# A Fourier-mixing and feed-forward kernel: first batch of x loaded in partition halves on two queues, column copies on another engine, last spill split by rows

## The chip, the cores and the metric

The kernel runs on one core of one Trainium2 chip. The core has a matrix engine (TensorE, PE in the profile; its weight loads are PEld), a vector engine (VectorE, DVE), a scalar engine (ScalarE, ACT), GpSimd (POOL) and SyncE (SP), which here only starts transfers. Engines run in parallel, each works through its own instruction stream in order, and semaphores make one wait for another. Transfers are started from the streams of SP, ACT or POOL and run on 16 shared DMA engines. The metric is the device time of one execution in microseconds (us), as the median over several runs.

## What is computed

```python
batch, seq, dim = (8, 3008, 256)
X = np.fft.fft(x, axis=1)
X = np.fft.fft(X, axis=2)
x = X.real.reshape(24064, 256)
h = x @ w_in                                  # 256 -> 2048
g = h * (1.0 / (1.0 + np.exp(-1.702 * h)))
out = g @ w_out                               # 2048 -> 256
```

A two-dimensional Fourier transform of each of eight batches, its real part, and a two-layer network on every row, all in float32.

## The kernel before

The Fourier transform is done with matrix products. The sequence of 3008 = 47 * 64 is split: a first stage mixes over 47 groups of rows, its result goes out to memory (`Td`, the "spill", line 289) and comes back with another axis on the partitions (`t4`, the "fill", line 295), and a second stage (`stage2`, line 314) mixes over 64. The transform over the 256 columns is folded into the weights: `fold_w` (line 418) multiplies w_in with a cosine table and leaves `wcs`. The main loop then runs 384 steps (8 batches, 3 blocks of rows, 2 halves, 8 pairs of 128 hidden units), each with the products of `hidden` (line 448), an activation, and the products of `product` (line 515). The next batch's first stage runs between the steps of the batch before it.

The first batch has no batch before it, so its first stage stands alone at the start of the kernel, and the change is there. It goes like this.

- `w0`, the mixing table (128 partitions, 800.5 KB), is loaded from ACT's stream (line 589) and scaled into a second copy `w0o` by ACT (line 600).
- `x[0]` lies in `xt` as 32 slots of 256 columns. Partitions 0 to 63 hold one half of the rows (`half` 0) and 64 to 127 the other. It is loaded by `load_first` (line 225) in four calls of eight slots each: slots 0 to 8, 24 to 32, 8 to 16, 16 to 24. One call starts four transfers of 32 partitions and 256 KB: partitions 0-31, 32-63, 64-95, 96-127, in that order. Fourteen of the 16 start from SP and two (slots 24 to 32, half 0) from ACT.
- Behind them SP starts `small` (the other tables), then the weight pieces `raw` `in 0` and `in 1` of 1 MB each (lines 594, 339).
- `warm(7)` (line 278) issues products whose result nobody reads.
- `fold_first(g)` (line 233) works on four slots: ACT copies two columns of each (line 235, 128 x 8 elements), DVE makes sums and differences of columns (line 237, two instructions). The order of the g is 0, 7, 1, then 6, 2, then 5, 3, then 4.
- `mix_first(k)`, k = 0 to 3 (line 240), is the mixing on PE: 32 products of 64 x 64 weights in two phases (64 entries in the profile), with two one-column copies on ACT between the phases (line 248). The first phase of mix k cannot begin before the sum and the column copy of the last g that it needs: g = 1, 2, 3, 4 for k = 0, 1, 2, 3. Afterwards ACT copies the two result banks back to `xt` (line 264).
- After k = 1, 2, 3 `spill` writes finished slots to `Td`, one transfer for each half of the partitions. The last one starts from SP and ACT. Then `fill(0, 0, 4)` reads rows 0 to 512 of `Td`, which are what rows m = 0 to 16 of every mix produced.
- Then the first weight piece is rounded. `bounds` puts two passes on ACT (lines 362, 363) and one on POOL (line 360), `round_in` three on DVE (lines 373 to 376), `finish_in` one on POOL (line 380). Four more `warm` products follow, and `fold_w(0)`, the correction `rotate` (lines 301, 302), and `stage2` of block 0, with which the main loop starts. The other seven weight pieces are rounded between the first steps of the main loop.

The order on every engine is the order in which the code issues instructions (`manual_schedule`). Eight semaphores are used in rotation for transfers started from SP and ACT together, so a ninth such transfer waits until the first has landed, and so on. Transfers started from POOL have eight others.

Of the kernel before, what the change touches and what calls it, by code (L numbers as in the profile page):

```python
# [35 lines left out]
NJ = NB // 2  # L36
NM = 48
# [9 lines left out]
def view(ap, offset, *dims):  # L47
    return bass.AP(ap.tensor, ap.offset + offset, [list(d) for d in dims])


def free(ap, offset, *dims):
    return bass.AP(ap.tensor, ap.offset + offset, [list(ap.ap[0])] + [list(d) for d in dims])
# [57 lines left out]
def kernel(ctx: ExitStack, tc, x, w_in, w_out, tab1, tab2, out):  # L110
    nc = tc.nc
    B, S, D = x.shape
    DF = w_in.shape[1]
    H = D // 2
# [17 lines left out]
    Td = [nc.dram_tensor(f"Td{b}", (NG * 128, D), F32, kind="Internal").ap() for b in range(B)]  # L132
# [17 lines left out]
    def bank(name):  # L150
        return psm.tile([128, 512], F32, tag="mm", name=name)
# [6 lines left out]
    xt = xp.tile([128, NJ, D], F32, tag="x", name="xt")  # L158
# [63 lines left out]

    room = {}

    def load_first(lo, hi, engines):
        for half in range(2):
            for g in range(2):
                eng, p = engines[2 * half + g], 64 * half + 32 * g
                eng.dma_start(out=xt[p:p + 32, lo:hi, :].rearrange("p j d -> p (j d)"),
                              in_=view(x, (NB * (NA - 32) * g + NJ * half + lo) * D, [NB * D, 32], [1, (hi - lo) * D]))  # L230

    def fold_first(g):

        t, e = xt[:, 4 * g:4 * g + 4, :], room[g]
        nc.scalar.copy(free(e, 0, [D, 4], [H, 2]), free(t, 0, [D, 4], [H, 2]))
        for at, op in ((1, ALU.add), (H + 1, ALU.subtract)):
            nc.vector.tensor_tensor(e[:, :, at:at + H - 1], t[:, :, 1:H], free(t, D - 1, [D, 4], [-1, H - 1]), op=op)

    def mix_first(k):


        ks = k, 7 - k
        ps = [bank("ps1") for _ in ks]
        for phase in range(2):
            if phase:

                for n in range(2):
                    nc.scalar.copy(af2[:, n:n + 1], ps[n][:, D + n * (H + 1):D + n * (H + 1) + 1])
            for at in range(4)[::-1 if phase else 1]:
                r, even = divmod(at, 2)  # L250
                for half in (phase, 1 - phase):
                    n = half ^ phase
                    for c in range(2):
                        jj = 4 * ks[n] + 2 * r + c
                        c0, c1 = (0, H + 1) if even ^ half ^ phase else (H + 1, D)
                        slot, first = ((NB - jj) % NJ if half else jj), c0 == 0
                        w, m = (w0o, jj) if jj and not first else (w0, jj or ENDS[1 - first])
                        rows_ = slice(64 * half, 64 * half + 64)
                        nc.tensor.matmul(ps[n][64 * c:64 * c + 64, r * D + c0:r * D + c1], lhsT=mat(w, m, rows_),  # L259
                                         rhs=room[slot // 4][rows_, slot % 4, c0:c1], start=(phase == 0 and at == 0),  # L260
                                         stop=(phase == 1), skip_group_check=True)
        for n in range(2):
            to = placed(ks[n])
            nc.scalar.copy(xt[:, to:to + 2, :].rearrange("p j d -> p (j d)"), ps[n][:])  # L264

    def placed(k):
        return 2 * k if k < 4 else 16 + 2 * k
# [6 lines left out]
    def warm(n):  # L274

        ps = bank("warm")
        for _ in range(n):
            nc.tensor.matmul(ps[:], lhsT=wcs[0][:, 0:128], rhs=wcs[0][:, 0:512], start=True, stop=True)

    def spill(b, ks=None, engines=(nc.sync, nc.sync)):  # L280

        for c, eng in enumerate(engines):
            src, at = xt[64 * c:64 * c + NM], 16 * c * D
            if ks is None:
                eng.dma_start(out=view(Td[b], at, [NJ * D, NM], [1, 16 * D]),
                              in_=src[:, 0:16, :].rearrange("p q d -> p (q d)"))
                continue
            (k0, n), k1 = ks, 8 - sum(ks)
            eng.dma_start(out=view(Td[b], at + 2 * k0 * D, [NJ * D, NM], [2 * (k1 - k0) * D, 2], [1, 2 * n * D]),
                          in_=free(src, placed(k0) * D, [(placed(k1) - placed(k0)) * D, 2], [1, 2 * n * D]))  # L290

    def fill(b, a0=0, a1=NG):
        if a0 == 0:
            t4t[b] = tp.tile([128, NG, D], F32, tag="t4", name="t4")
        nc.sync.dma_start(out=t4t[b][:, a0:a1, :], in_=Td[b].rearrange("(a p) d -> p a d", p=128)[:, a0:a1, :])
# [41 lines left out]
    def load_in(n, eng):  # L337
        t = raw["in", n] = cv.tile([128, 1024, 2], U32, tag="raw", bufs=3, name="raw")
        eng.dma_start(out=t[:].rearrange("p (i f) w -> p i (f w)", i=2),
                      in_=w_in[:, n * 512:(n + 1) * 512].bitcast(U32).rearrange("(i p) f -> p i f", p=128))  # L340

    def load_out(n, eng):
        t = raw["out", n] = cv.tile([128, 1024, 2], U32, tag="raw", bufs=3, name="raw")
        eng.dma_start(out=t[:].rearrange("p (f n) w -> p f (n w)", f=4),
                      in_=w_out[4 * n * 128:(4 * n + 4) * 128, :].bitcast(U32).rearrange("(p f) n -> p f n", p=128))
# [3 lines left out]
    def bounds(key, first=False):  # L349


        hi, lo = raw[key][:, :, 1].bitcast(F32), raw[key][:, :, 0]
        g = sp.tile([128, 1024], F32, tag="s", bufs=3, name="g")
        m = cv.tile([128, 1024], F32, tag="m", name="m")
        r = cv.tile([128, 1024], U32, tag="r", bufs=2, name="r")
        if first:
            nc.vector.tensor_tensor(g[:], hi, hi, op=ALU.mult)
        else:
            nc.scalar.activation(g[:], hi, ACTF.Square)
        nc.gpsimd.tensor_scalar(m[:], hi, scalar1=TOP, scalar2=-TOP, op0=ALU.min, op1=ALU.max)  # L360

        nc.scalar.activation(r[:].bitcast(F32), lo, ACTF.Copy, scale=2.0 ** -29, bias=2.0 ** 23)  # L362
        nc.scalar.activation(r[:], r[:].bitcast(F32), ACTF.Copy, bias=-2.0 ** 23)  # L363
        pre[key] = g, m, r
# [36 lines left out]
    def finish_in(n):  # L401
        last["in", n]()
# [184 lines left out]
    nc.vector.memset(wcs[0][:, 0:512], 1.0)  # L587
    nc.vector.memset(ones[:], 1.0)
    nc.scalar.dma_start(out=w0, in_=tab1[:, 0:n0 + 1])
    load_first(0, 8, (nc.sync,) * 4)  # L590
    load_first(24, 32, (nc.scalar, nc.scalar, nc.sync, nc.sync))
    load_first(8, 16, (nc.sync,) * 4)
    load_first(16, 24, (nc.sync,) * 4)
    nc.sync.dma_start(out=small[:], in_=tab2)
    load_in(0, nc.sync)
    load_in(1, nc.sync)
    warm(7)

# [2 lines left out]
    for k, need in enumerate(((0, 7, 1), (6, 2), (5, 3), (4,))):  # L601
        for g in need:
            fold_first(g)
        mix_first(k)
        if k:
            spill(0, ((0, 2), (2, 1), (3, 1))[k - 1], (nc.sync, nc.scalar if k == 3 else nc.sync))
    fill(0, 0, 4)
    load_out(0, nc.sync)
    bounds(("in", 0), True)
    round_in(0)  # L610
    finish_in(0)
    warm(4)
    bounds(("in", 1))
    fold_w(0)
    fill(0, 4, NG)
# [13 lines left out]
    n = len(steps)  # L629
# [17 lines left out]
    for b in range(B):  # L647
        t0 = b * NBLK * NF
        late = 0 if b else 3
        if b + 2 < B:  # L650
            at(t0 + 10, turn, b + 2)
        if b + 1 < B:
            for c in range(NCH):
                at(t0 + 7 + 2 * c + late, fold1, b + 1, c, nc.gpsimd)
                if c % 2:
                    at(t0 + 8 + 2 * c + late, mix1, b + 1, c // 2)
            at(t0 + 24 + late, spill, b + 1)
            at(t0 + 29 + late, fill, b + 1)
            if b + 2 < B:
                at(t0 + 33 + late, load_x, b + 2)  # L660
            at(t0 + 36 + late, rotate, b + 1)
        for blk in range(NBLK):
            nxt = (b, blk + 1) if blk + 1 < NBLK else (b + 1, 0)
            if nxt[0] < B:
                at(t0 + blk * NF + 8, stage2, *nxt)
                at(t0 + blk * NF + 12, nyquist, *nxt)
# [49 lines left out]
```

## Time and profile before

| | us |
|---|---|
| median of 7 runs | 1939.94 (1939.35 to 1941.69) |
| the profiled execution, its own time | 1938.24 |
| its span in the profile | 1936.2 |
| PE busy | 1909.4 (99% of the span) |
| PEld / POOL / DVE / ACT busy | 1671.8 / 755.1 / 1410.0 / 674.9 |
| mean granted PE clock | 0.992 of full |
| first result of the last mix of batch 0 copied (line 264) | 36.22 |
| first products of the main loop (line 448) | 50.41 |

Except for the first 90 us or so, PE is busy almost without a gap. The profile has several views that are used below: the chain of work that ended last (start, length, engine, tile, line), the table of stages (start:end, length, then the busy time of PE, PEld, DVE, ACT and POOL with the number of instructions in brackets, then the granted PE clock, the mean busy share of the DMA engines, and GB/s moved), and the timeline (start, length from first start to last end, engine, line, operation, out<-in, count, and in brackets the idle time before it with what ended it).

### The profile page before, as it was taken

The numbers are of one execution on the slowest core, as the hardware profiler recorded it, in microseconds if no ns is written. First come the engines' busy times: TensorE is split into PE (matmuls) and PEld (weight loads), VectorE is DVE, ScalarE is ACT, GpSimd is POOL, SyncE is SP. The second block draws the span as 40 slices with busy tenths as digits, with TensorE's granted clock in tenths as the row PEclk, the third lists the DMA queues.
The fourth block names the chain that finished last, engine by engine and source line by source line (L and its number), as shares of the span: only waits on it lengthen the run. The fifth ranks groups of instructions, "written<-read, shape, count | busy, mean of one in ns | idle before, by whom it ended". The sixth has DMA issues, their size and how long they took to land.

```text
span 1936.2 us, 29491 instructions
## 1 busy us (share of the span) xinstructions
PE 1909.4 (99%) x10820; PEld 1671.8 (86%) x10820; DVE 1410.0 (73%) x2924; ACT 674.9 (35%) x936; POOL 755.1 (39%) x1045
## 2 busy tenths in 40 slices
PE   7899999999999999999999999999999999999998
PEld 4598888988889888898889888898888988889887
DVE  3777777777778667877777777777777777777776
ACT  3733333333333333333333333333333333333332
POOL 1565223642245322462225522355223643223222
PEclk7999999999999999999999999999999999999999
DMA  8740460227203362025522262221720223202201
GB/s 235 205 70 11 91 82 13 49 51 116 17 12 58 49 109 17 20 51 93 65 24 49 32 102 41 25 49 43 115 24 13 18 45 59 17 12 27 17 12 22
DMA packets 145520, 104.53 MB, mean 54 GB/s; under 512 B 105443, under 2 KB 128259, under 8 KB 143681
## 3 DMA queue, kind: packets, MB, share of 16 engines
q1 hardware_dynamic: 143360, 100.84, 31.1%
q10 hardware_dynamic: 2016, 1.81, 0.3%
q8 instruction: 86, 1.41, 0.3%
q14 instruction: 58, 0.47, 0.1%
HBM read 59.36 MB, written 48.01 MB: 55 GB/s over the span
## 4 chain that ended last, share of the span: by engine, by line
PE 96%; DMA 1%; POOL 1%; issue 1%; DVE 1%; ACT 1%; ACTq 0%; POOLq 0%; DVEq 0%
PE po L515 59%; PE pa L448 17%; PE pb L448 17%; PE ps L210 1%; PE ps L314 1%; DMA xt<-in_x_dram 1%; PE ps L259 1%; PE psw L418 0%; POOL wst L380 0%; POOL wo L380 0%; PE ps L214 0%; ACT xt L264 0%; POOL m L360 0%; ACT r L362 0%; ACT r L363 0%
## 5 line engine op out<-in xcount | busy, mean ns | idle before, releaser
L489 POOL TENSOR_TENSOR s<-h 128x256 f32<-128x256 f32 (+1 forms) x376 | 270.0, 718 | 1094.1 <-ACT h L477 1029.0
L515 PE MATMUL po<-s,wt 128*128 128x256 f32 (+1 forms) x2256 | 599.7, 375 | 0.0
L452 ACT COPY v<-pa 128x512 f32<-128x512 f32 (+1 forms) x384 | 222.0, 578 | 1062.8 <-PE pa L448 1062.8
L462 DVE TENSOR_TENSOR h<-v,pb 128x512 f32<-128x512 f32 (+1 forms) x384 | 259.1, 675 | 398.2 <-PE pb L448 393.5
L515 PEld LDWEIGHTS po<-s,wt 128*128 128x128 f32 x2256 | 428.6, 190 | 48.3
L515 PE MATMUL po<-h,wo 128*128 128x256 f32 (+1 forms) x1632 | 469.7, 375 | 0.1
L477 ACT ACTIVATE h<-h 128x1024 f32<-128x1024 f32 (+1 forms) x384 | 400.8, 1044 | 18.0 <-DVE h L472 15.3
L448 PE MATMUL pa<-pq,wcs 128*128 128x256 f32 (+1 forms) x1536 | 393.8, 379 | 2.6 <-ACT wcs L420 1.3
L448 PE MATMUL pb<-pq,wcs 128*128 128x256 f32 (+1 forms) x1536 | 387.9, 375 | 2.1 <-DVE dif L465 1.8
L515 PEld LDWEIGHTS po<-h,wo 128*128 128x128 f32 x1632 | 310.0, 190 | 36.0 <-issue 0.5
L448 PEld LDWEIGHTS pa<-pq,wcs 128*128 128x128 f32 x1536 | 286.8, 190 | 51.2 <-issue 11.2
L465 DVE SCALAR_TENSOR_TENSOR dif<-nb,af,pb 128x256 f32<-128x256 f32 (+1 forms) x768 | 328.3, 469 | 2.2 <-DMA af<-row 2.2
L448 PEld LDWEIGHTS pb<-pq,wcs 128*128 128x128 f32 x1536 | 291.5, 190 | 36.2 <-DVE dif L465 2.2
L490 POOL TENSOR_TENSOR s<-h 128x256 f32<-128x256 f32 (+1 forms) x376 | 276.4, 735 | 0.0
L472 DVE TENSOR_TENSOR h<-pa,dif 128x512 f32<-128x512 f32 (+1 forms) x448 | 265.4, 604 | 13.2
L515 PE MATMUL po<-s,wo 128*128 128x256 f32 (+1 forms) x752 | 220.3, 375 | 0.0
L515 PE MATMUL po<-h,wt 128*128 128x256 f32 (+1 forms) x752 | 220.3, 375 | 0.0
L493 DVE TENSOR_TENSOR s<-h,s 128x256 f32<-128x256 f32 (+1 forms) x376 | 206.0, 548 | 12.9
L492 DVE TENSOR_TENSOR s<-s,h 128x256 f32<-128x256 f32 (+1 forms) x376 | 179.2, 476 | 4.3 <-POOL s L489 4.3
L515 PEld LDWEIGHTS po<-s,wo 128*128 128x128 f32 x752 | 142.9, 190 | 16.1
L515 PEld LDWEIGHTS po<-h,wt 128*128 128x128 f32 x752 | 142.9, 190 | 16.1
L320 DVE STREAM_TRANSPOSE pq<-ps 128x256 f32<-128x256 f32 x96 | 34.6, 417 | 59.4 <-PE ps L314 59.4
(66 smaller groups left out, 741.5 us busy)
## 6 DMA issues: line engine op xcount, KB each, us to landing
out_dram<-os SPq DMA_DIRECT2D x284, 64.0 KB
Td<-xt SPq DMA_DIRECT2D x14, 768.0 KB
t<-Td SPq DMA_DIRECT2D x7, 1536.0 KB
xt<-in_x_dram SPq DMA_DIRECT2D x14, 512.0 KB
xt<-Xr SPq DMA_DIRECT2D x14, 512.0 KB
nb<-pq SPq DMA_DIRECT2D x23, 256.0 KB
out_dram<-os SPq DMA_DIRECT2D x96, 56.0 KB
Xr<-in_x_dram SPq DMA_DIRECT2D x7, 752.0 KB
```

Of the source, the lines that this page charges most:

```text
L320: nc.vector.transpose(free(pq[:], cs * 512 + u * RUN, [256, 2], [NU * RUN, 4], [1, RUN]), free(ps[u][:], cs * 256, [128, 2], [32, 4], [1, ...
L448: nc.tensor.matmul(ps[:, i * 256:i * 256 + n], lhsT=wcs[cs][:, f * 128:(f + 1) * 128], rhs=pq[:, cs, ks], start=True, stop=True)
L452: nc.scalar.copy(two(v[:], n), two(pa[:], n))
L462: nc.vector.tensor_tensor(two(h[:], n), two(v[:], n), two(pb[:], n), op=ALU.add)
L465: nc.vector.scalar_tensor_tensor(dif[:, i * 256:i * 256 + n], nb[:, ks], af2[:, f:f + 1], pb[:, i * 256:i * 256 + n], op0=ALU.mult, op1=AL ...
L472: nc.vector.tensor_tensor(free(h[:], 512 + at + m - 1, [256, 2], [RUN, blocks], [-1, m]), *ins, op=ALU.add)
L477: nc.scalar.activation(g, g, ACTF.Gelu_apprx_sigmoid)
L489: eng.tensor_tensor(s1, a21, a22, op=ALU.add)
L490: eng.tensor_tensor(s3, a11, a21, op=ALU.subtract)
L492: eng.tensor_tensor(s2, s1, a11, op=ALU.subtract)
L493: eng.tensor_tensor(s4, a12, s2, op=ALU.subtract)
L515: nc.tensor.matmul(pot[q][:, i, :n], lhsT=lhs, rhs=rhs, start=(p == 0 and i == 0 and f == 0), stop=(p == NP - 1), skip_group_check=True)
```

## The change

`load_first` no longer takes a list of engines: half 0 (partitions 0 to 63) starts from SP, half 1 (64 to 127) from POOL, in turn, so eight transfers on each. The column copies of `fold_first` move from ACT to POOL. The weight piece `in 0` is started before `small`. The second transfer of the spill after k = 2 starts from ACT too. The spill after k = 3 is made in two parts, rows 0 to 16 and rows 16 to 48 (two transfers each), with `fill(0, 0, 4)` between them; four transfers in place of two. One more `warm` product follows.

```diff
-    def load_first(lo, hi, engines):
-        for half in range(2):
-            for g in range(2):
-                eng, p = engines[2 * half + g], 64 * half + 32 * g
+    def load_first(lo, hi):
+        for g in range(2):
+            for half, eng in enumerate((nc.sync, nc.gpsimd)):
+                p = 64 * half + 32 * g
                 eng.dma_start(out=xt[p:p + 32, lo:hi, :].rearrange("p j d -> p (j d)"),
...
-        nc.scalar.copy(free(e, 0, [D, 4], [H, 2]), free(t, 0, [D, 4], [H, 2]))
+        nc.gpsimd.tensor_copy(free(e, 0, [D, 4], [H, 2]), free(t, 0, [D, 4], [H, 2]))
...
-    def spill(b, ks=None, engines=(nc.sync, nc.sync)):
+    def spill(b, ks=None, engines=(nc.sync, nc.sync), m0=0, m1=NM):
         for c, eng in enumerate(engines):
-            src, at = xt[64 * c:64 * c + NM], 16 * c * D
+            src, at = xt[64 * c + m0:64 * c + m1], (NJ * m0 + 16 * c) * D
...
-    load_first(0, 8, (nc.sync,) * 4)
-    load_first(24, 32, (nc.scalar, nc.scalar, nc.sync, nc.sync))
-    load_first(8, 16, (nc.sync,) * 4)
-    load_first(16, 24, (nc.sync,) * 4)
+    for lo in (0, 24, 8, 16):
+        load_first(lo, lo + 8)
+    load_in(0, nc.sync)
     nc.sync.dma_start(out=small[:], in_=tab2)
-    load_in(0, nc.sync)
     load_in(1, nc.sync)
...
         if k:
-            spill(0, ((0, 2), (2, 1), (3, 1))[k - 1], (nc.sync, nc.scalar if k == 3 else nc.sync))
-    fill(0, 0, 4)
+            for m in ((0, NM),) if k < 3 else ((0, 16), (16, NM)):
+                spill(0, ((0, 2), (2, 1), (3, 1))[k - 1], (nc.sync, nc.scalar if k > 1 else nc.sync), *m)
+                if k == 3 and m[0] == 0:
+                    fill(0, 0, 4)
...
-    warm(4)
+    warm(5)
```

More of the change, by code (lines that the diff above doesn't have):

```diff
@@ L278, in warm @@
             nc.tensor.matmul(ps[:], lhsT=wcs[0][:, 0:128], rhs=wcs[0][:, 0:512], start=True, stop=True)
-    def spill(b, ks=None, engines=(nc.sync, nc.sync)):
+    def spill(b, ks=None, engines=(nc.sync, nc.sync), m0=0, m1=NM):
         for c, eng in enumerate(engines):
-            src, at = xt[64 * c:64 * c + NM], 16 * c * D
+            src, at = xt[64 * c + m0:64 * c + m1], (NJ * m0 + 16 * c) * D
             if ks is None:
-                eng.dma_start(out=view(Td[b], at, [NJ * D, NM], [1, 16 * D]),
+                eng.dma_start(out=view(Td[b], at, [NJ * D, m1 - m0], [1, 16 * D]),
                               in_=src[:, 0:16, :].rearrange("p q d -> p (q d)"))
@@ L288, in spill @@
             (k0, n), k1 = ks, 8 - sum(ks)
-            eng.dma_start(out=view(Td[b], at + 2 * k0 * D, [NJ * D, NM], [2 * (k1 - k0) * D, 2], [1, 2 * n * D]),
+            eng.dma_start(out=view(Td[b], at + 2 * k0 * D, [NJ * D, m1 - m0], [2 * (k1 - k0) * D, 2], [1, 2 * n * D]),
                           in_=free(src, placed(k0) * D, [(placed(k1) - placed(k0)) * D, 2], [1, 2 * n * D]))
```

## The prediction

> **What bounds the kernel now.** The page first: PE is busy for 99% of the span and makes up 96% of the chain that ended last. Nothing in the main loop is edited, so only the start can move. I therefore read the chain up to 50 us, then the stages that it names.
>
> ```profile
> 26.30 0.59 ACT xt L264
> 26.89 0.22 ACT e L235 x2
> ...
> 27.16 3.89 PE ps L259 x56
> ...
> 36.22 1.08 ACT xt L264 x2
> ...
> 37.74 1.14 ACT r L362
> ...
> 40.04 2.38 POOL wst L380
> ...
> 42.46 3.71 PE psw L418 x8
> ```
>
> Before 20 us the chain is transfers of x. Then it alternates: a mix on PE, ACT's two copies of its result, ACT's column copies for the next mix, the next mix. The column copies have had their data for long; they merely stand behind the result copies in ACT's stream. After the fourth mix it goes over ACT's and POOL's rounding passes to the weight products, not over the spill and the fill: the fill's reader (line 301) ran at 46.00, right behind the weight products in PE's stream. What follows (rounding of the other pieces on DVE, POOL and ACT until about 90 us, then PE) depends on work, not on the clock on the wall. So I take a shift of the fourth mix to go through to the end in full.
>
> The timeline of DVE and PE shows when x lands:
>
> ```profile
> 12.21 1.29 DVE L237 TENSOR_TENSOR first<-xt 128x508 f32<-128x508 f32 x2 [10.69 <-DMA xt<-in_x_dram]
> 14.48 2.48 DVE L237 TENSOR_TENSOR first<-xt 128x508 f32<-128x508 f32 x4 [0.98 <-DMA xt<-in_x_dram]
> ...
> 19.24 1.28 DVE L237 TENSOR_TENSOR e<-xt 128x508 f32<-128x508 f32 x2 [1.08 <-DMA xt<-in_x_dram]
> 23.73 3.68 DVE L237 TENSOR_TENSOR e<-xt 128x508 f32<-128x508 f32 x6 [3.20 <-DMA xt<-in_x_dram]
> ```
>
> The four groups land at T0 = 12.2, T1 = 14.48, T2 = 19.24, T3 = 23.73. Mix 0 starts at 16.51, which is T1 + 2.03 (three DVE instructions of 0.68). Mixes 1 to 3 start at 21.88, 27.16 and 32.30 and the last ends at 36.2; one mix takes 3.9 to 4.0.
>
> The table of stages shows the transfers:
>
> ```profile
> 6.00:7.50 1.50, 1.50 (x5) 0.74 (x4) 0.00 (x0) 0.63 (x1) 0.00 (x0) 1.00 0.99 208
> 8.00:10.00 2.00, 1.20 (x3) 0.19 (x1) 0.00 (x0) 0.50 (x1) 0.00 (x0) 1.00 0.98 291
> 10.50:22.00 11.50, 5.51 (x72) 4.18 (x76) 6.25 (x10) 2.12 (x9) 0.00 (x0) 0.53 1.02 223
> 23.50:28.50 5.00, 4.40 (x65) 3.63 (x63) 3.98 (x7) 1.61 (x6) 0.24 (x1) 0.50 1.03 412
> ```
>
> The last three numbers are the granted PE clock, the busy share of the DMA engines and GB/s. The engines count as fully busy in all four, at very different rates. By the bytes that each queue had moved (view of the queues), SP stood at partitions 32-63 and ACT at 0-31 or 32-63 from 6.0 to 7.5: two queues in one half, 208 GB/s. From 8 to 10 SP was at partitions 64-127 and ACT at 32-63: two queues in opposite halves, 291. Then SP alone with 32 partitions at a time: 223. Last, transfers over all 128 partitions: 412. The PE clock is worth a look too: it falls from 1.00 to 0.50 in the third row.
>
> ```profile
> 7.96:11.37 3.41, 1.24 (x3) 0.19 (x1) 0.00 (x0) 0.54 (x1) 0.00 (x0) 0.99 1.02 269
> 35.26:38.67 3.41, 3.41 (x27) 2.04 (x20) 0.00 (x0) 2.01 (x3) 0.00 (x0) 0.51 0.17 34
> ```
>
> The clock fell at 11.4 after a stretch with PE 36% busy and came back at 38.7, in the warm products. All four mixes ran at half clock.
>
> **Part 1, the loads.** The trace has no pair of queues that stays in opposite halves, except 8 to 10 us. I take its 291 GB/s; the bounds are 223 (no gain) and 412 (as 128 partitions). In the first 6 us 1.28 MB were moved, and I leave that. T1 needs w0 and two groups, 0.82 + 2.10 = 2.92 MB; T2 3.97; T3 5.01. Before, 5.01 MB had been moved at 22.1 and T3 was 23.73, so 1.6 lies between the mean and the last engine. At 291: T1 = 6 + 1.64/0.291 + 1.6 = 13.2, T2 = 16.8, T3 = 20.4. At 412: 11.6, 14.1, 16.7. At 223: 15.0, 19.7, 24.3.
>
> [...]
>
> **Part 2, issue on POOL.** The trace has no transfer issued by POOL. The nearest rows are SP's: 0.31 to 0.65 for one of these loads, 2.6 for the longest (two of line 164 in 5.17). I take 1.0, an estimate: the geometric middle of 0.4 (the median of these loads) and 2.6. Eight end at 0.74 + 8 = 8.7, before T1, and hide behind the loads. The column copies are queued behind all eight; that cover is gone from 1.5 each on.
>
> **Part 3, column copies on POOL.** ACT loses eight instructions of 0.2. A POOL copy lies between 0.10 (MEMSET of 128x1) and 0.73 (TENSOR_TENSOR of 128x256); I take 0.2, beside DVE's two instructions of 1.3 for the same g, so nothing. What goes is the detour over ACT: 1.36 between mixes 1 and 2 (25.80 to 27.16) and 1.25 between 2 and 3, and mix 1 no longer waits for ACT's copies of mix 0 either. The result copies (1.07) now run beside the next mix's first phase (1.7). One cost may appear: DVE's line 373 took 1.71 at 83.84 while POOL's line 380 ran until 84.46, against 1.22 at 30.42 with POOL idle, so the two can hold each other up. If POOL is shut out for all of DVE's run, mix 0 starts at T1 + 2.7 and mix 2 at T3 + 3.9: 1.2 later at the end.
>
> **Part 4, spill, fill, order.** The second issue on ACT (0.37 as the row of line 289, plus a gap) stands ahead of line 362, on the path: +0.4. The one after k = 2 fits into the first phase of mix 3 (1.07 + 0.37 < 1.7). SP's later half of the spill and the big fill are read only at the fourth step of the main loop, 80 us: nothing. The earlier fill was not on the path: nothing. `in 0` ahead of `small` lands sooner than the 28.2 of before; both are needed after 31. The fifth warm product (two passes, each 0.43 at full clock and 0.85 at half, by the distance of the passes before and after 38.7) fits: the last mix to the weight products is 6.3 + 0.4; with 3.4 us at half clock (one stretch as in the rows above) the ten passes need 4 x 0.85 + 6 x 0.43 = 6.0. After two such stretches they need 7.7 and cost 1.0.
>
> **Sum at 291 GB/s.** Mix 0 starts at 13.2 + 2.0 = 15.2 and ends at 19.2. Mix 1 needs the sum of g = 2: DVE is through with g = 7, 1 and 6 at 13.2 + 2.5 + 1.3 = 17.0 and with that sum at 17.7, so mix 1 runs from 19.2 to 23.1. Mix 2 needs T3 + 1.84 = 22.2, so it follows at once, to 27.0, and mix 3 to 30.9. Against 36.2 that is 5.3, less 0.4: 4.9 gained. The profiled span of 1936.2 becomes 1931.3. That execution was 1.7 below the median; the difference carries over: 1935.0. At 412 GB/s: mix 0 at 13.6, the last ends at 29.3, 6.5 gained, 1933.4.
>
> **Rivals.** 0.2% is 3.9 us, about what a measurement of this kernel tells from no change, and decides between faster (under 1936.1) and same.
>
> A: the halves do not help and the loads stay at 223 GB/s. For it: "fully busy" engines throughout. Mix 0 starts at 17.0, mix 1 ends at 24.9, mix 2 waits for T3 + 1.84 = 26.1, the last ends at 33.9: 2.3 - 0.4 = 1.9 gained, 1938.0. POOL shut out by DVE has a smaller price, 1936.2.
>
> B: the clock comes back during the mixes, now that they run without a gap but for the 0.32 between phases. For it: 35.26 to 38.67 brought it back with a gap of 0.29. Against: 2.2 us of that window were warm products, and no window of mixes alone did. From mix 2 on two mixes would take about 2.5 instead of 3.9: 1932.2; from mix 1 on 1931.3.
>
> C, the other side: POOL needs 2.6 for each issue. Then its stream is free at 21.5, the copies of the first three g end at 22.1, and mix 0 starts there: the last ends at 37.8, 1.6 + 0.4 = 2.0 lost, 1941.9. It decides from 2.35 each; 3.3 would make it slower by over 0.2%. Against: the same transfer took SP 0.4.
>
> **Chances.** Forecast (1933.4 to 1936.5) 0.45, B 0.20, A and the shut-out together 0.22, C and what I have not seen 0.13. Faster takes B and nearly all of the forecast: 0.62; same the rest, A and half of C: 0.31; slower 0.07. The likeliest is 1935.0. For 8 in 10 I reach from B's 1931.3 to somewhat above A, 1939.0.
>
> **What would show it.** Right: over 280 GB/s from 8 us to the last x, mix 0 before 15.5, mixes 0.3 apart at most, line 362 0.8 behind the last result copy, the gap of 1.3 gone. Wrong: x rows on POOL's queue that trail SP's; POOL's column copies later than T1 + 1; mixes that still wait for DVE or POOL; or later stages (60 to 90 us) that wait for a transfer, so that the shift does not arrive.

## The result and the profile after

The changed kernel takes 1934.33 us in the median of 13 runs (1932.09 to 1935.92), the kernel before 1940.04 in the median of 31 runs beside it (1937.56 to 1942.03). The ratio is 0.9969, with a 95% interval of 0.9962 to 0.9977: 5.7 us faster. The profiled execution of the changed kernel took 1935.57, 1.2 above its median, while that of the kernel before was 1.8 below its own. The two profiles therefore differ by only 2.6, and most of what follows is about where the rest of the 5.7 hides.

The first lines of the page, and of its queue part (packets, MB, share):

```profile
span 1933.6 us, 29514 instructions
...
q0 software_dynamic: 384, 2.10, 0.4%
```

Half of the first batch of x, 2.10 MB, now runs on POOL's queue. The chain that ended last, over the mixes and the first weight products (start, length, engine, tile, line):

```profile
1.97 0.97 POOL xt L229 x2
2.94 11.29 DMA xt<-in_x_dram
...
15.65 0.61 POOL e L235
...
16.34 5.89 PE ps L259 x92
...
22.25 0.17 ACT af L248
22.42 0.04 issue
22.46 1.15 PE ps L259 x31
23.61 0.02 issue
23.63 0.94 ACT xt L264 x2
24.57 0.04 issue
24.61 0.17 ACT af L248
24.78 0.04 issue
24.82 1.12 PE ps L259 x26
...
28.88 0.08 ACT xt L264
...
29.98 0.36 ACTq L289
30.34 0.04 issue
30.38 0.87 ACTq L289
31.25 0.05 issue
31.30 1.15 ACT r L362
...
36.02 5.12 PE psw L418 x8
```

The first transfer in the chain is one that POOL started. The last column copy ahead of mix 0 stands in the chain too, but none (line 235) stands between the mixes any more. Between the result copies of the last mix (line 264) and the rounding pass of line 362 stand two transfer issues of ACT where there was one. The weight products take 5.12 where they took 3.71. The clock tells why, in the table of stages of the same kernel (start:end, length, busy PE, granted PE clock, DMA share, GB/s):

```profile
10.00:12.00 2.00, 0.00 (x0) 0.90 1.00 295
18.45:21.87 3.42, 3.42 (x63) 0.51 0.97 291
32.10:35.52 3.42, 1.27 (x3) 0.99 0.16 45
35.52:38.93 3.41, 2.91 (x4) 0.51 1.00 381
42.35:45.76 3.41, 1.38 (x35) 0.99 1.07 395
45.76:49.17 3.41, 3.41 (x7) 0.50 0.91 360
```

The clock falls at 11.6 (at 11.4 before), but is back at 21.9, in the second mix. It falls again at 35.5, after a stretch in which PE waited for the rounding, and once more at 45.8. At about 56 it is back at 1.00 and stays there until the last 4 us, in which PE has no more work. The timeline shows the groups of x landing (DVE) and what POOL does with them:

```profile
10.80 1.29 DVE L237 TENSOR_TENSOR first<-xt 128x508 f32<-128x508 f32 x2 [9.26 <-DMA xt<-in_x_dram]
14.31 2.48 DVE L237 TENSOR_TENSOR first<-xt 128x508 f32<-128x508 f32 x4 [2.23 <-DMA xt<-in_x_dram]
...
21.23 4.63 DVE L237 TENSOR_TENSOR e<-xt 128x508 f32<-128x508 f32 x6 [2.04 <-DMA xt<-in_x_dram]
```

```profile
1.28 4.08 POOL L229 DMA_DIRECT2D xt<-in_x_dram  x8 [0.82 <-POOLq L700]
10.85 0.70 POOL L235 COPY first<-xt 128x8 f32<-128x8 f32 x1 [5.49 <-DMA xt<-in_x_dram]
14.34 1.31 POOL L235 COPY first<-xt 128x8 f32<-128x8 f32 x2 [2.80 <-DMA xt<-in_x_dram]
```

T1 is 14.31 where it was 14.48, T3 is 21.23 where it was 23.73. One reason why T1 gained so little is that the two queues did not advance together. SP's queue (q1) moved its first bytes before 2.0 us, POOL's (q0) only after 5.5; by 6.0 us it was 0.40 MB on SP's and 0.05 on POOL's. What the two had moved by 13.0 us (queue: packets, MB, share):

```profile
q1 hardware_dynamic: 253, 1.43, 40.2%
q0 software_dynamic: 191, 1.07, 29.0%
```

The first two groups are 1.05 MB on each queue. SP's queue had passed that before 11.0 us (1.12 MB there), POOL's only just before 13.0. At the end of x it is the same: SP's queue had its 2.10 MB by about 18.0, POOL's by about 20.5.

Cut at five marks, the two profiles compare like this (starts in us):

| stretch | before | after | difference |
|---|---|---|---|
| start to first result copy of the last mix (line 264) | 36.22 | 28.88 | -7.34 |
| from there to line 362 | 1.52 | 2.42 | +0.90 |
| from there to the copy of line 302, behind the weight products | 10.53 | 11.61 | +1.08 |
| from there to the fourth weight products (line 418, at 84.90) | 39.40 | 41.99 | +2.59 |
| from there to the end | 1848.5 | 1848.7 | +0.2 |

The mixes are 7.3 earlier, and 4.6 of it is given back by 85 us. The last row was 1848.5 to 1848.8 in all fourteen profiles of this study, whatever the kernel. So the start alone decides, up to the fourth weight products.

### The profile page after: what moved, and what is told of

The parts are those of the page before. It is cut to its first block, busy times and chain, and to the rows that moved or that the text cites. A ratio compares the mean times of both kernels' runs of the same rounds, so it can differ in the third digit from the quotient of the medians.

```text
span 1933.6 us, 29514 instructions
## 1 busy us (share of the span) xinstructions
PE 1908.4 (99%) x10822; PEld 1671.7 (86%) x10822; DVE 1408.3 (73%) x2924; ACT 673.2 (35%) x928; POOL 763.9 (40%) x1061
## 3 DMA queue, kind: packets, MB, share of 16 engines
q8 instruction: 86, 1.41, 0.3%
## 4 chain that ended last, share of the span: by engine, by line
PE 96%; POOL 1%; issue 1%; DMA 1%; DVE 0%; ACT 0%; ACTq 0%; POOLq 0%
PE po L515 59%; PE pa L448 17%; PE pb L448 17%; PE ps L210 1%; PE ps L314 1%; DMA xt<-in_x_dram 1%; PE ps L259 0%; PE psw L418 0%; POOL wst L380 0%; POOL wo L380 0%; PE ps L214 0%; POOL m L360 0%; ACT r L362 0%; ACT xt L264 0%; ACT r L363 0%
## 5 line engine op out<-in xcount | busy, mean ns | idle before, releaser
L472 DVE TENSOR_TENSOR h<-pa,dif 128x512 f32<-128x512 f32 (+1 forms) x448 | 265.5, 604 | 13.2
```

The costliest lines, as they stand in the source:

```text
L472: nc.vector.tensor_tensor(free(h[:], 512 + at + m - 1, [256, 2], [RUN, blocks], [-1, m]), *ins, op=ALU.add)
```

## The experiments

Four groups of kernels were run in five rounds each, every group on one chip beside the kernel before (groups 3 and 4 on the same one). A median is compared with the before of its own group.

| kernel | median (lowest to highest, runs) | ratio to before (95%) | span in its profile | last mix copied, line 264 | line 302 to fourth weight products |
|---|---|---|---|---|---|
| group 1, before 1939.8 | | | | | |
| copies_only | 1937.54 (1935.62 to 1938.20, 11) | 0.9989 (0.9980 to 0.9998) | 1935.7 | 32.87 | 42.5 |
| loads_only | 1939.53 (1938.96 to 1942.62, 11) | 1.0004 (0.9995 to 1.0012) | 1939.1 | 37.50 | 41.1 |
| spill_whole | 1934.82 (1932.68 to 1936.37, 9) | 0.9975 (0.9966 to 0.9984) | 1932.9 | 30.85 | 41.6 |
| same_half | 1935.94 (1933.34 to 1940.18, 12) | 0.9987 (0.9979 to 0.9996) | 1933.9 | 32.41 | 40.7 |
| group 2, before 1939.65 | | | | | |
| after_again | 1933.89 (1933.46 to 1937.36, 7) | 0.9973 (0.9962 to 0.9984) | 1932.6 | 30.61 | 41.2 |
| warm8 | 1934.19 (1931.89 to 1936.08, 8) | 0.9972 (0.9962 to 0.9982) | 1930.1 | 29.84 | 39.3 |
| warm13 | 1935.05 (1933.32 to 1936.30, 11) | 0.9977 (0.9968 to 0.9986) | 1931.4 | 30.33 | 40.2 |
| steady | 1933.66 (1931.72 to 1936.65, 6) | 0.9974 (0.9962 to 0.9985) | 1931.4 | 30.44 | 40.4 |
| group 3, before 1939.46 | | | | | |
| after_third | 1933.49 (1932.72 to 1936.68, 9) | 0.9974 (0.9965 to 0.9984) | 1930.7 | 29.85 | 40.0 |
| hold | 1932.68 (1932.26 to 1933.16, 5) | 0.9965 (0.9952 to 0.9977) | 1931.1 | 30.81 | 39.2 |
| group 4, before 1938.82 | | | | | |
| hold_split | 1934.60 (1933.04 to 1935.65, 11) | 0.9977 (0.9969 to 0.9986) | 1933.2 | 29.93 | 42.3 |
| hold_again | 1933.84 (1932.02 to 1936.29, 12) | 0.9978 (0.9969 to 0.9986) | 1930.8 | 30.54 | 39.2 |

**copies_only.** The kernel before with the column copies on POOL and nothing else.

```diff
-        nc.scalar.copy(free(e, 0, [D, 4], [H, 2]), free(t, 0, [D, 4], [H, 2]))
+        nc.gpsimd.tensor_copy(free(e, 0, [D, 4], [H, 2]), free(t, 0, [D, 4], [H, 2]))
```

> The kernel before with one edit: the column copies of fold_first go to POOL. Theory (two independent gains, the detour over ACT and the rate of the loads): the groups of x land as before (12.2, 14.5, 19.2, 23.7), mix 1 starts when its data is there (about 20.6), mix 2 at T3 + 1.9 = 25.6, mixes 2 and 3 follow each other without a gap, the last ends at 33.5 at half clock: 2.7 gained, median about 1937.3. Rival 1 (the loads do it all): no change, 1940.0. Rival 2 (the clock does it: mixes without a gap bring the clock back): the granted clock returns to 1.0 during the mixes as in the changed kernel, the last mix ends before 32, median below 1936.5.

Measured 1937.54, 2.3 below before. Its timeline, PE's third and fourth mix and DVE's last group:

```profile
26.12 5.29 PE L259 MATMUL ps<-e,wt 64*64 64x129 f32 x92 [2.52 <-POOL e L235]
```

```profile
24.09 3.68 DVE L237 TENSOR_TENSOR e<-xt 128x508 f32<-128x508 f32 x6 [3.33 <-DMA xt<-in_x_dram]
```

The clock came back in the second mix here too (two mixes without a gap). Then PE stood idle for 2.5, because the last group of x landed only at 24.09, and the clock fell once more: the granted clock is 0.75 on average over 26.12 to 29.50. POOL is named as what ended the wait, but its copy had been waiting for the transfer. So the copies alone turn the wait for ACT into a wait for the loads.

**loads_only.** The kernel before with the new `load_first` on SP and POOL and with `in 0` ahead of `small`; the column copies stay on ACT, the spill and the warm products are as before.

```diff
-    load_first(0, 8, (nc.sync,) * 4)
-    load_first(24, 32, (nc.scalar, nc.scalar, nc.sync, nc.sync))
-    load_first(8, 16, (nc.sync,) * 4)
-    load_first(16, 24, (nc.sync,) * 4)
-    nc.sync.dma_start(out=small[:], in_=tab2)
+    for lo in (0, 24, 8, 16):
+        load_first(lo, lo + 8)
     load_in(0, nc.sync)
+    nc.sync.dma_start(out=small[:], in_=tab2)
```

> The kernel before with only the new loads (half 0 from SP, half 1 from POOL, weight piece in 0 ahead of small); column copies stay on ACT, spill and warm products as before. Theory: x moves at about 295 GB/s, the last group lands at 21.2, but every mix waits again for ACT's two result copies and its column copies (1.3 each); mix 0 at 16.3, the mixes at a distance of 5.2, the last ends at about 35.5 at half clock: 0.7 gained, median about 1939. Rival (the loads do it all): as the changed kernel, 1934.3. Rival (the last group sets the pace): 2.5 gained, 1937.5.

Measured 1939.53 against 1939.8: no gain. The timeline of PE:

```profile
28.45 4.68 PE L259 MATMUL ps<-e,wt 64*64 64x129 f32 x64 [0.60 <-ACT e L235]
33.59 4.25 PE L259 MATMUL ps<-e,wt 64*64 64x129 f32 x60 [0.46 <-ACT e L235]
```

With the column copies behind the result copies on ACT, each mix waits for ACT again, the starts are 5.1 to 5.4 apart, and the clock stays at 0.50 to the warm products. Four such mixes from T1 + 2 take longer than the loads do at either rate, so only T1 counts, and T1 was 15.77, later than the 14.48 of before. The copies alone give 2.3 and the loads alone nothing that can be seen; together, in spill_whole of the same group, they give 5.0. Each removes the wait that hides the other's gain.

**same_half.** The changed kernel with the two queues in one half: SP 0-31 beside POOL 32-63, then 64-95 beside 96-127.

```diff
-        for g in range(2):
-            for half, eng in enumerate((nc.sync, nc.gpsimd)):
+        for half in range(2):
+            for g, eng in enumerate((nc.sync, nc.gpsimd)):
```

> The changed kernel with another pairing: SP loads partitions 0-31 while POOL loads 32-63, then SP 64-95 while POOL loads 96-127, so two queues work in the same half; bytes, transfers and queues are as many. Theory (a half has a limit of its own): 210 to 230 GB/s instead of 295, the last group lands at about 24, the last mix ends 2.5 to 3 later, about 1937. Rival (two queues are faster wherever they write): 295 GB/s and 1934.3. Rival (the rate does not matter since the mixes are bound by PE or ACT): the rate falls, but the time stays at 1934.3.

The table of stages from 10.5 to 20 us (busy PE, clock, DMA share, GB/s), first of this kernel, then of copies_only, in which SP alone moves x in this stretch (the two transfers from ACT are through by then), then of the kernel spill_whole below, whose loads are those of the changed kernel:

```profile
10.50:20.00 9.50, 1.69 (x23) 0.68 1.01 232
```

```profile
10.50:20.00 9.50, 3.89 (x57) 0.69 1.02 217
```

```profile
10.50:20.00 9.50, 2.94 (x38) 0.63 1.01 251
```

Two queues in one half move 232, 7% more than one queue (217); in opposite halves they move 251 (loads_only: 252), another 8%, on the same chip. So the second queue and the pairing of halves have about an equal part in the rate here. From 8 to 18 us the rate was 296 in the first profile of the changed kernel, 253 to 279 in the later profiles with these loads, and 234 in same_half. The time of same_half is 1935.94, 1.1 above spill_whole (which differs in the last spill too), in the direction of the theory but with overlapping intervals.

**spill_whole.** The changed kernel with the last spill in one piece and the fill behind it.

```diff
-            for m in ((0, NM),) if k < 3 else ((0, 16), (16, NM)):
-                spill(0, ..., *m)
-                if k == 3 and m[0] == 0:
-                    fill(0, 0, 4)
+            spill(0, ...)
+    fill(0, 0, 4)
```

> The changed kernel with the last spill in one part (one transfer from SP, one from ACT) and the fill behind it. Theory: the two ACT issues (0.36 and 0.87) become one of 0.37, line 362 starts 0.9 sooner after the last result copy, and the fill is not on the path: 0.9 faster than the changed kernel, about 1933.4. Rival (the split brings the fill forward and that counts): 0.5 to 1.5 slower, line 301 then waits for the fill.

The timeline of ACT behind the last mix, first of this kernel, then of the changed kernel in a second profile (after_again):

```profile
30.85 1.07 ACT L264 COPY xt<-ps 128x512 f32<-128x512 f32 x2 [1.13 <-PE ps L259]
31.95 0.36 ACTq L289 DMA_DIRECT2D Td<-xt  x1
32.36 1.14 ACT L362 ACTIVATE r<-raw 128x1024 f32<-128x1024 uint32 x1 [0.44 <-ACT xt L264]
```

```profile
30.61 1.07 ACT L264 COPY xt<-ps 128x512 f32<-128x512 f32 x2 [1.13 <-PE ps L259]
31.72 0.84 ACTq L289 DMA_DIRECT2D Td<-xt  x2
32.60 1.12 ACT L362 ACTIVATE r<-raw 128x1024 f32<-128x1024 uint32 x1 [0.92 <-ACT xt L264]
```

One issue puts 0.44 between the copies and line 362, two put 0.92 there (1.35 in the first profile after, where the second issue took 0.87). In the medians 1934.82 stands beside 1934.33 and 1933.89 of the changed kernel: the split is worth nothing that can be seen, and its 0.5 shows in the trace alone.

**after_again** is the changed kernel unchanged; **warm8** issues eight instead of five warm products behind the last mix; **warm13** issues 13 instead of 7 at the very start; **steady** is spill_whole with seven instead of five behind the last mix, and one before and one behind the first `stage2`.

```diff
-    warm(5)
+    warm(8)
```

```diff
-    warm(7)
+    warm(13)
```

```diff
-    warm(5)
+    warm(7)
...
+    warm(1)
     stage2(0, 0)
+    warm(1)
```

> The changed kernel once more, beside the other runs of this group on one chip, as their base. Theory: 5 to 6 under the kernel before, about 1934.3. Open is the rate of the paired loads, which the profile of the changed kernel showed at 295 GB/s and the two kernels with opposite halves in the first group at about 254: if the chip or the moment sets it, this run lies anywhere between and the last group lands between 21.2 and 23.3; if the column copies' place sets it, it is 295 again.

> The changed kernel with eight warm products in place of five before the first weight product. Theory (the clock after the mixes costs): eight take 6.9 at full clock and fill the 7.1 between the last mix and the first weight product, the clock does not fall at 35, the first weight product takes 3.7 where it took 5.1, and the next steps keep the full clock: 1 to 2.5 faster than the changed kernel in executions where the clock had come back in the mixes, 1932 to 1933.5 in the median. Rival 1 (those losses are hidden by the rounding on POOL and DVE): no difference. Rival 2 (in executions where the clock is still halved, eight products hold PE up by 1 to 3): slower, 1935 to 1936.

> The changed kernel with thirteen warm products in place of seven at the start, which keep PE busy to about 14.4, so that the clock does not fall at 11.6 and mix 0 runs at full clock (2.3 instead of 3.9). Theory (the last group of x is the bound once the mixes run at full clock): mix 0 ends 1.6 sooner, mixes 1 and 2 then wait for their data, the end moves by under 0.7, and the new idle may make the clock fall: 1933.5 to 1935. Rival (the clock in the first mixes is the bound): 1.5 to 3 faster, 1931.5 to 1933.

> The changed kernel with the last spill in one part, seven warm products instead of five before the first weight product, and one more on either side of the first stage2, where PE was idle. Theory: line 362 starts 0.5 to 0.9 sooner, the clock stays full from the mixes on: 1.5 to 3 faster than the changed kernel, 1931.5 to 1933. Rival (nothing after the mixes is bound by PE): 0.5 to 0.9 from the spill alone, 1933.5. Rival (added products delay the work behind them on PE): not faster than the changed kernel.

The second profile of the changed kernel lost its time in another place than the first. It has no fall of the clock behind the last mix, but one in the wait for the third weight products. The timeline of PE, after_again and then warm8:

```profile
65.59 5.40 PE L418 MATMUL psw<-wst,small 128*128 128x512 f32 x8 [1.96 <-POOL wst L380]
```

```profile
29.78 7.13 PE L278 MATMUL warm<-wcs 128*128 128x512 f32 x16
36.75 3.60 PE L418 MATMUL psw<-wst,small 128*128 128x512 f32 x8
50.19 3.70 PE L418 MATMUL psw<-wst,small 128*128 128x512 f32 x8 [0.95 <-POOL wst L380]
64.83 3.70 PE L418 MATMUL psw<-wst,small 128*128 128x512 f32 x8 [2.13 <-POOL wst L380]
```

In warm8 all weight products ran at full clock, and its span of 1930.1 is 3.5 below that of the first profile after. But its median is the changed kernel's: it was one lucky execution, as the 1931.89 at the low end of its runs shows. Warm13 kept the clock up to about 18.8 us (1.00 from 17 to 18 us, 0.71 on average from 18 to 20), but its first mix started no sooner (17.38), since T1 sets it, and the median is not lower. Steady, expected at 1931.5 to 1933, took 1933.66; in its profile the clock fell in the wait for the third weight products all the same.

**hold** fills the waits before the second and third weight products as well, on top of steady; **after_third** is the changed kernel beside it.

```diff
-    warm(7)
+    warm(8)
...
         if t in early:
+            if t in (1, 3):
+                warm((t + 1) // 2)
             fold_w(early[t])
```

> After with the last spill in one piece and idle products where PE waits in the start: eight instead of five before the first weight products, one before and one behind the first block of the second stage, one before the second and two before the third weight products (PE was idle 0.95 and 1.96 to 2.13 there). Theory: what is left of the scatter of the changed kernel is the clock that falls in these waits. Then no profile row shows a clock under 1.0 from the third mix on, the third weight products take 3.7 and not 5.4, the span from the first copy of line 302 to the fourth weight products is 39.4 to 39.8, and the median is 1931.5 to 1933, 1 to 2.5 below the changed kernel in the same rounds, with a narrower spread (under 3). Rival 1: the idle products delay the weight products behind them by as much as they save (they run when the data is there already): 39.4 becomes 40.5 or more, median as the changed kernel's. Rival 2: the scatter comes from the transfers of x and not from the clock: the clock stays and the times still spread over 4.

> The changed kernel once more, as the mark for the run beside it: 1933.5 to 1934.5 in the median. Its profile tells whether the transfers of x run at 296 GB/s between 8 and 18 us, as in the first profile, or near 255, as in the second. If the clock in the waits makes the scatter, its span is about 1930 plus 1.7 for each weight product that falls to half clock.

The profile of hold has a granted clock of 1.00 in every stage from 25 us on, the stretch from line 302 to the fourth weight products is 39.2, as short as in warm8, and its five runs lie within 0.9 of each other. That looked like the answer: the scatter of the changed kernel is the clock falling in waits, and with the waits filled it is gone. After_third, with 40.0 in that stretch and no fall either, spread over 4.0 in nine runs. Two more kernels were run to see whether this holds.

**hold_split** is hold with the last spill split as in the changed kernel; **hold_again** is hold unchanged.

```diff
-            spill(0, ...)
-    fill(0, 0, 4)
+            for m in ((0, NM),) if k < 3 else ((0, 16), (16, NM)):
+                spill(0, ..., *m)
+                if k == 3 and m[0] == 0:
+                    fill(0, 0, 4)
```

> The kernel before this one (idle products in the waits) with the last spill in two parts again and the fill between them, as in the changed kernel. With the clock held the times should lie within 1 of each other, so that a small cost can be seen: theory, the second issue on ACT puts line 362 0.4 to 0.5 later behind the last result copy (0.9 instead of 0.44) and the median is 0.4 to 0.9 above the one with the spill in one piece. Rival: the earlier fill pays somewhere and the median is the same or lower. If the spread is again 4 as in the changed kernel, the narrow one was chance.

> The version with idle products and the spill in one piece once more, on the same chip as the split one: median 1932.3 to 1933.1, all runs within 1 to 1.5; if it is 1933.5 or more, or spreads over 3, it is no better than the changed kernel.

It does not hold. Hold_again spread over 4.3 in twelve runs, so the narrow five were chance, and 1933.84 is no better than the changed kernel. The split costs 0.8 in these two medians, of the size that was expected, but within the scatter. The profile of hold_split shows one more place where the clock can fall. Its timeline of PE, then the stages (busy PE, clock, DMA share, GB/s):

```profile
78.38 1.89 PE L448 MATMUL pb<-pq,wcs 128*128 128x256 f32 x4 [2.15 <-DVE dif L465]
80.06 4.58 PE L515 MATMUL po<-h,wo 128*128 128x256 f32 x16
```

```profile
76.60:80.00 3.40, 1.62 (x4) 0.79 0.32 100
80.00:83.40 3.40, 3.40 (x12) 0.70 1.07 151
```

PE waited 2.15 for DVE in front of line 448, a wait that no idle product covers, and the clock fell there: it was 0.79 and 0.70 on average in these two rows, and the sixteen products of line 515 took 4.58 against 3.62 in hold_again. The clock fell at this place in copies_only, loads_only and spill_whole too (0.74, 0.93 and 0.87 on average from 80 to 85 us; line 515 took 5.30, 4.46 and 4.19). No version tried is faster than the changed kernel beyond the intervals. All 17 runs of hold and hold_again have a median of 1933.4, all 29 of the changed kernel 1934.02.

## Why the prediction was right, and where its steps were not

The forecast of 1935.0 was 0.7 above the median, but that the number came so close is partly luck. The sum has 4.9 from mixes that run at half clock without the detour over ACT. The detour did go. But mix 0 started 1.1 later than the sum has it (first profile), the later mixes ran at full clock, and what this gained was partly given back behind them, in waits and falls of the clock for which the sum has no term.

- **Loads, the rate.** 291 GB/s was taken; the first profile shows 296 from 8 to 18 us, the later ones 253 to 279. Rival A (the halves do not help) is out as far as the mechanism goes, since same_half ran at 232 where opposite halves ran at 251. The runs show 251 against 217 for one queue on the same chip from 10.5 to 20 us, 16% more, and 282 once, in the first profile: a gain, but in most profiles less than what was taken.
- **Loads, T1 and T3.** This is the step that failed. T1 was to be 13.2 and was 14.31, T3 20.4 and was 21.23, though the rate was reached. The sum counts the bytes of both queues together, as if both began at once ("In the first 6 us 1.28 MB were moved, and I leave that"). By that count the 2.92 MB of T1 had been moved at about 11.6, but T1 came 2.7 later, not the 1.6 that was read before the change. About half of the 2.7 is POOL's queue, which had its part of T1 only just before 13.0, while SP's had run ahead with bytes of later groups; the rest, about 1.4, lies between POOL's last bytes and the landing. "x rows on POOL's queue that trail SP's" was the first of the prediction's own signs of being wrong, and it came true; "mix 0 before 15.5", a sign of being right, did not. At 253 to 279 GB/s T1 was even later than before (14.8 to 15.8). The new loads brought the first group and the last two sooner, and not the one that starts mix 0: in the first profile it started at 16.34 and not at 15.2, in the others later.
- **Issue on POOL.** Taken 1.0 each; eight took 4.08, so 0.51. Rival C is out. The 2.6 it rests on was read from a row of two issues of line 164 in 5.17 that has waiting in it: each of these issues took 0.61 to 0.94 in the profile before. But the loads did not quite hide the eight issues: the last one ended at 5.36, and until 6.0 POOL's queue had moved 0.05 MB. Whether the issues or the load of `w0`, which ended at about the same time, held the queue back was not tested.
- **Column copies on POOL.** Taken 0.2; they took 0.66 to 0.76, more than three times ACT's. They were hidden all the same, but with no slack left: the last one that mix 0 needs ended at 16.26 and stands in the chain, and mix 0 started at T1 + 2.03, as before the change. The shut-out by DVE did not come: three copies ran from 14.34 to 16.25, and DVE's four sums beside them from 14.31 to 16.79.
- **The clock.** "mix 1 runs from 19.2 to 23.1", at half clock, was the forecast; the mechanism of rival B, given 0.20, is what happened, though not its time of 1932.2. With the copies on POOL the clock was back at 1.00 by the third mix in each profile of such a kernel (in copies_only it fell again in that mix). In the first profile mix 0 took 4.0 to its first result copy and those of the others followed 3.3, 2.4 and 2.9 apart, by then bound by ACT: the result copies, the issue of line 289 and the copies of line 248 stand in the chain between them. In after_again and after_third the third mix still waited for T3 (0.42 and 0.28 idle). The last mix was done 2.0 sooner than the 30.9 of the forecast in the first profile, and 0.3 and 1.0 sooner in these two, in spite of the later T1. Over all runs the mean granted clock shows it too: in the median of the runs 0.992 to 0.993 before, 0.992 with the loads alone, 0.994 with the copies alone, 0.996 after. The profiled execution had 0.993, the lowest of the 13. The times go with it. Of the 90 runs of the kernel before in the four groups, the 40 with a mean clock of 0.992 have a median of 1939.95, and the seven with 0.997 one of 1935.8. The seven runs of the changed kernel with 0.997 (of its 29) have 1933.5. At the same mean clock the two kernels are thus 2.3 apart, so by this estimate some 3.4 of the 5.7 come with the clock and not with the shift that the sum is made of. It is no more than an estimate, because a mean does not tell where the clock was low.
- **Second issue on ACT.** +0.4 taken, +0.5 to 0.9 measured.
- **"I take a shift of the fourth mix to go through to the end in full."** True from the fourth weight products on (1848.5 to 1848.8 everywhere), not between. There the clock and the waits gave back part of what the mixes gained: it fell behind the mixes (35.5 to 38.9, then 45.8 to 56 in the first profile) or at 65 to 71 (after_again, same_half, steady, copies_only), or near 80 (spill_whole, copies_only, loads_only, hold_split). The stretch from line 302 to the fourth weight products, 39.4 in the profile before, is 40.4 to 42.5 in these. "The fifth warm product fits" was therefore too narrow: in the first profile the products ended at 33.4, and PE idled to 36.0. At full clock they were over too soon, and the clock fell in the wait that they were meant to bridge (0.51 from 35.52 to 38.93, behind 2.65 idle); in after_again and after_third it did not fall there (2.21 idle, and the weight products took 3.70).

The sum as measured in the first profile is the table of the result: -7.3 at the last mix, +0.9 for the two issues, +3.7 for the clock and the waits behind it, with the +0.2 of the last row together -2.6. In after_third it is -6.4 at the last mix (29.85 against 36.22), +0.5 to line 362, -0.3 to line 302 and +0.6 to the fourth weight products. With the last row that is -5.5 in the span (1930.7 against 1936.2), although its mixes ended 1.0 later than in the first profile. In after_again it is -5.6, +0.5, -0.3, +1.8 and in all -3.6. Between these three profiles, what an execution gains depends more on what it loses behind the mixes than on when the mixes end.

What stays open: why the loads ran at 296 GB/s in one profile and at 253 to 279 in the others (it is not the chip alone: the four profiles of group 2, with the same loads on one chip, span 253 to 279), what held POOL's queue back at the start, and what sets the 4 us of scatter that remains when most waits are filled. Hold_split shows that one more fall of the clock can make 1.7 of it (1.89 and 4.58 against the 1.13 and 3.62 of hold_again); the rest of the 3.1 by which its stretch up to the fourth weight products is longer lies in waits. The runs with the lower mean clock are slower in the changed kernel as well (the ten at 0.995 or less took 1934.4 to 1937.4, the seven at 0.997 1933.4 to 1933.8), but at 0.996 they still run from 1932.1 to 1935.9, so the clock is not all of it.

## What to carry to other kernels

Removing one of two waits in series can be worth nothing, and removing both more than the sum (nothing and 2.3 alone, 5.0 together): look up what ends the wait after the one you take away. When work is shared between two queues, look at each queue's own progress: the sum of their bytes hid that one of them began over 3 us after the other. An idle stretch of about 2 us on TensorE cost more than its length in some profiles and not in others: behind 1.96 idle the third weight products took 5.40 in after_again, behind 2.13 they took 3.70 in warm8. So measure the clock in each stretch and not only the waits. A narrow spread over five runs is no proof of a stable kernel; the same kernel spread over 4.3 in the next twelve.

## What the runs showed of the hardware

- The clock changed at 11.63, 21.87, 35.52, 38.93 and 45.76 in the first profile after. The shortest distance is 3.41, the others are 3, 4 and 2 times that. It fell after stretches of this length with PE 33%, 37% and 40% busy (1.14 of 3.41, 1.27 of 3.42 and 1.38 of 3.41). The stretches 45.76 to 49.17 and 49.17 to 52.58 were both fully busy in the table of stages (3.41 of 3.41), and the clock stayed at 0.50 through both and at 0.51 to 56.00; the mixes from 18.45 to 21.87 were as busy (3.42 of 3.42), and behind them it was 1.00. The busy share alone thus does not tell when the clock comes back; what does was not settled.
- A column copy of 128 x 8 elements takes POOL 0.66 to 0.76 and ACT 0.2.
- DVE's six sums of the last groups took 4.63 instead of 3.68 in the changed kernel and 4.59 in loads_only, which has no column copies on POOL; copies_only, which has them, took 3.68. In the changed kernel, POOL's line 360 ran beside them (23.30 to 24.71), because `in 0` now lands before the sums are over. One sum took 1.63 there and the others at most 0.69, and line 360 took 1.41 where it took 1.11 later (at 35.94). In loads_only line 360 ran beside the sums too (from 25.48) and took 1.38. Both thus took longer where they ran side by side, but the chain of the first profile does not pass through it.
- Of two queues that were given transfers from about 0.75 (SP) and 1.28 us (POOL) on, SP's had moved 0.40 MB by 6.0 us and POOL's 0.05. In the first profile SP's stayed about 0.3 MB ahead until its half of x was through at 18.0 us.
